# Layer norm, Fourier filter and gated bilinear layer on one core: all sixteen row tiles transposed on TensorE instead of twelve by DMA

## The chip, the cores and the metric

The kernel runs on one core of a Trainium2 chip. The metric is the device time of one execution in microseconds (us). Before the change it is 196.71 us, the median of three runs that lie between 196.61 and 196.75 us.

## The reference

The inputs are bf16. A_x has shape (1, 2048, 640). The reference normalises each of its 2048 rows and adds three terms: the input itself, a filter in the two-dimensional Fourier domain, and a gated bilinear layer.

```python
m = jnp.mean(x, axis=-1, keepdims=True); v = jnp.var(x, axis=-1, keepdims=True)
xn = (x - m) / jnp.sqrt(v + 1e-5)
X = jnp.fft.rfft2(xn.astype(jnp.float32), axes=(-2, -1)) * (w_r + 1j * w_i)   # w: (2048, 321)
a = jnp.fft.irfft2(X, s=(2048, 640), axes=(-2, -1)).astype(jnp.bfloat16)
g = jnp.einsum("bsd,df->bsf", xn, w_gate)     # (640, 1536)
u = jnp.einsum("bsd,df->bsf", xn, w_up)
b = jnp.einsum("bsf,fd->bsd", g * u, w_down)  # (1536, 640)
return x + a + b
```

## The kernel before

**Tiles.** The 2048 rows are sixteen row tiles of 128 rows, held in SBUF in one array of memory (the `arena` of the profile) beside the weights and all intermediate results. PSUM is one tensor `ps` of eight banks.

**Tasks.** `_build` describes the program as tasks: a name, the engines that may run it, a duration that only a planner uses, a function that emits its instructions, and what it reads and writes. `_PLAN` is a list of triples (number of the task, engine, PSUM bank), and `replay` walks through it. So the order of the instructions on each engine, the engine itself where there are two, and the banks are written out by hand in that list. `compute_waits` then derives the semaphore waits. Every engine, SP too, executes its own list strictly in order.

**Names of tasks used below**, with the line that the profile shows, and the work of one task:

- `ld_...` (L675): a load or a store, issued by SP except for the first two on ACT. `ld_x1` to `ld_x3` bring row tiles 1 to 3, `ld_x4` tiles 4 to 7, `ld_x5` tiles 8 to 15; `ld_gw0_0` and `ld_gw0_1` the first gate and up weights, and so on; `ld_fd`, `ld_tf`, `ld_ti`, `ld_g` tables for the Fourier steps; `ld_w...` pieces of the filter; `ld_wd...` parts of w_down.
- Statistics of a row tile, in one of two ways. On DVE: two `bn` (L754) and an `ag` (L761). On ACT: `sm` (L736, the mean) and `sq` (L745, the sum of squares). `act_set` names those of the first four tiles that go to ACT: 2 and 3. Tiles 4 and 5 are on DVE, tiles 6 to 15 on ACT.
- `sd` (L770, L771, ACT): the standard deviation; `rs` (L778, DVE): its reciprocal; `mul` (L795, DVE): subtracts the mean and multiplies, in place. Tiles 0 to 3 have an `sd` each, later tiles one for two.
- `T0_b` (L814, TensorE): five 128x128 transposes of row tile b into PSUM, for tiles 0 to 3 only, and `eT0_b` (L682 on DVE, L681 on ACT), the copy to SBUF. For tiles 0 and 1 that copy is two instructions on DVE.
- `xt_b` (L802, SP): one DMA transpose of row tile b, for tiles 4 to 15. It takes no PSUM and no engine but SP's queue and the DMA engines.
- `GU_f_b_u` (L973 for the narrow ones, L951 for those 512 columns wide): the product of gate (u=0) or up (u=1) weights of column block f with the row tiles that start at b. `eG` is its copy out of PSUM (L681 ACT, L682 DVE), and `H` (L991, L993, DVE) multiplies the two.
- `S1` to `S5` (L857 to L892, DVE), `R_b` (L905, TensorE) and `eR_b`: the first Fourier steps on a row tile. `D`, `C`, `IA`, `I` (L1034, L1053, L1116, L1144) are the further Fourier steps on TensorE, `WM`, `SM`, `J`, `V` those on DVE, ACT and POOL.
- `ACC`, `IV` (L1221, L1233): the product with w_down and the last Fourier step, accumulated in one bank; `FIN` (L1242, L1260) adds the input, and `st_out` stores.
- `warm` (L714) is 42 matmuls on constants ahead of the first useful one, and `fill0` (L704) five more.

**Order around the change.** TensorE begins with

```
warm T0_0 fill0 T0_1 GU_0_0_1 GU_0_0_0 GU_0_1_0 GU_0_1_1 GU_2_0_1 T0_2 GU_2_0_0 T0_3 GU_2_1_0 ...
```

DVE's list begins with the statistics of tile 0, then `bn1`, `bn1`, and only then `rs_0`, `ag1`, `mul0`, `rs_1`, `mul1` and the copies of `T0_0` and `T0_1`. ACT's begins with `sd_0`, `sd_1`, `sm2`, `sq2`, `sm3`, `sd_2`, `sq3`, `sd_3`. SP issues all loads of x and of the gate and up weights first, then `xt4`, `xt7`, `ld_fd`, `xt5`, `xt6`, six filter pieces, and the other eight `xt` scattered among filter pieces and tables.

Of the kernel before, what the change touches and what calls it, by code (L numbers as in the profile page):

```python
# [400 lines left out]
def _d_act(n):  # L401
# [4 lines left out]
    (12, 1, -1), (19, 2, -1), (10, 0, 1), (0, 3, -1), (11, 4, -1), (13, 4, -1), (18, 2, -1), (20, 2, -1), (28, 2, -1),  # L406
    (27, 2, -1), (170, 1, -1), (14, 4, -1), (8, 3, -1), (21, 1, -1), (22, 2, -1), (29, 2, -1), (23, 2, -1), (30, 1, -1),
    (31, 2, -1), (32, 2, -1), (24, 0, 3), (25, 2, -1), (26, 2, -1), (9, 0, 7), (33, 0, 1), (34, 2, -1), (35, 2, -1),
    (181, 0, 0), (182, 2, -1), (36, 1, -1), (37, 1, -1), (15, 4, -1), (43, 1, -1), (38, 1, -1), (169, 4, -1), (179, 0, 6),
    (180, 2, -1), (39, 2, -1), (40, 2, -1), (183, 2, -1), (44, 1, -1), (45, 1, -1), (46, 2, -1), (47, 2, -1), (189, 0, 1),  # L410
    (191, 0, 0), (190, 1, -1), (192, 1, -1), (193, 2, -1), (172, 4, -1), (186, 0, 6), (171, 4, -1), (112, 2, -1), (187, 1, -1),
    (41, 0, 2), (42, 1, -1), (184, 0, 7), (185, 1, -1), (16, 4, -1), (54, 2, -1), (113, 2, -1), (48, 0, 6), (49, 1, -1),
    (62, 1, -1), (194, 0, 5), (196, 0, 3), (197, 1, -1), (195, 1, -1), (188, 2, -1), (198, 2, -1), (50, 2, -1), (51, 2, -1),
    (53, 2, -1), (114, 2, -1), (55, 2, -1), (52, 2, -1), (63, 1, -1), (206, 0, 2), (207, 1, -1), (64, 1, -1), (204, 0, 7),
    (205, 1, -1), (115, 2, -1), (173, 4, -1), (209, 0, 6), (174, 4, -1), (65, 1, -1), (210, 1, -1), (66, 1, -1), (67, 2, -1),
    (56, 1, -1), (57, 2, -1), (116, 2, -1), (199, 0, 3), (200, 1, -1), (70, 2, -1), (201, 0, 2), (202, 1, -1), (203, 2, -1),
    (58, 2, -1), (208, 2, -1), (17, 4, -1), (121, 2, -1), (72, 1, -1), (1, 4, -1), (211, 0, 7), (175, 4, -1), (212, 1, -1),
    (176, 4, -1), (177, 4, -1), (73, 1, -1), (117, 0, 2), (118, 1, -1), (119, 0, 5), (74, 1, -1), (213, 2, -1), (122, 2, -1),
    (68, 2, -1), (123, 2, -1), (75, 1, -1), (76, 1, -1), (77, 2, -1), (216, 0, 1), (217, 1, -1), (214, 0, 0), (215, 1, -1),
    (218, 2, -1), (221, 0, 2), (222, 1, -1), (78, 2, -1), (124, 2, -1), (219, 0, 3), (220, 1, -1), (223, 2, -1), (80, 2, -1),  # L420
    (224, 0, 4), (120, 1, -1), (225, 1, -1), (82, 1, -1), (60, 2, -1), (226, 0, 2), (227, 1, -1), (229, 0, 6), (230, 1, -1),
    (83, 1, -1), (84, 1, -1), (178, 4, -1), (231, 0, 5), (125, 2, -1), (128, 0, 6), (126, 0, 3), (129, 1, -1), (232, 1, -1),
    (228, 2, -1), (130, 2, -1), (233, 2, -1), (131, 2, -1), (59, 4, -1), (71, 4, -1), (2, 4, -1), (236, 0, 0), (237, 1, -1),
    (61, 4, -1), (85, 1, -1), (234, 0, 2), (127, 1, -1), (86, 1, -1), (235, 1, -1), (238, 2, -1), (132, 2, -1), (92, 1, -1),
    (241, 0, 6), (242, 1, -1), (239, 0, 7), (240, 1, -1), (93, 1, -1), (243, 2, -1), (133, 2, -1), (87, 2, -1), (246, 0, 4),
    (244, 0, 1), (245, 1, -1), (94, 1, -1), (247, 1, -1), (248, 2, -1), (134, 2, -1), (69, 4, -1), (249, 0, 6), (250, 1, -1),
    (95, 1, -1), (96, 1, -1), (97, 2, -1), (251, 0, 2), (252, 1, -1), (90, 2, -1), (253, 2, -1), (88, 2, -1), (98, 2, -1),
    (100, 2, -1), (254, 0, 7), (255, 1, -1), (256, 0, 3), (257, 1, -1), (438, 4, -1), (433, 4, -1), (259, 0, 4), (260, 1, -1),
    (258, 2, -1), (137, 0, 5), (139, 0, 0), (437, 4, -1), (435, 4, -1), (441, 4, -1), (472, 4, -1), (101, 4, -1), (91, 4, -1),
    (434, 4, -1), (470, 4, -1), (3, 4, -1), (135, 0, 2), (136, 1, -1), (143, 2, -1), (138, 1, -1), (102, 1, -1), (261, 0, 7),  # L430
    (262, 1, -1), (79, 4, -1), (89, 4, -1), (141, 0, 3), (269, 0, 2), (263, 2, -1), (142, 1, -1), (140, 1, -1), (266, 0, 5),
    (267, 1, -1), (144, 2, -1), (270, 1, -1), (264, 0, 4), (265, 1, -1), (268, 2, -1), (145, 2, -1), (271, 0, 5), (274, 0, 1),
    (103, 1, -1), (104, 1, -1), (272, 1, -1), (273, 2, -1), (81, 4, -1), (442, 4, -1), (466, 4, -1), (146, 2, -1), (105, 1, -1),
    (106, 1, -1), (275, 1, -1), (279, 0, 4), (280, 1, -1), (276, 0, 0), (277, 1, -1), (278, 2, -1), (107, 2, -1), (147, 2, -1),
    (110, 2, -1), (108, 2, -1), (468, 4, -1), (469, 4, -1), (281, 0, 6), (282, 1, -1), (286, 0, 7), (287, 1, -1), (283, 2, -1),
    (284, 0, 3), (152, 0, 4), (148, 0, 6), (153, 1, -1), (99, 4, -1), (431, 4, -1), (440, 4, -1), (432, 4, -1), (4, 4, -1),
    (683, 4, -1), (109, 4, -1), (111, 4, -1), (473, 4, -1), (156, 2, -1), (429, 4, -1), (439, 4, -1), (467, 4, -1), (471, 4, -1),
    (149, 1, -1), (285, 1, -1), (288, 2, -1), (157, 2, -1), (150, 0, 0), (289, 0, 2), (151, 1, -1), (154, 0, 4), (291, 0, 6),
    (296, 0, 0), (290, 1, -1), (292, 1, -1), (155, 1, -1), (293, 2, -1), (158, 2, -1), (301, 0, 2), (299, 0, 6), (300, 1, -1),
    (294, 0, 4), (295, 1, -1), (304, 0, 7), (306, 0, 6), (6, 4, -1), (297, 1, -1), (298, 2, -1), (159, 2, -1), (160, 2, -1),  # L440
    (305, 1, -1), (307, 1, -1), (309, 0, 0), (310, 1, -1), (302, 1, -1), (303, 2, -1), (311, 0, 7), (312, 2, -1), (308, 2, -1),
    (163, 0, 5), (164, 1, -1), (167, 0, 1), (161, 0, 3), (162, 1, -1), (168, 2, -1), (314, 0, 0), (315, 2, -1), (313, 2, -1),
    (165, 0, 4), (316, 0, 6), (317, 2, -1), (166, 1, -1), (446, 0, 2), (447, 1, -1), (448, 2, -1), (474, 0, 0), (443, 0, 4),
    (444, 2, -1), (445, 1, -1), (324, 0, 7), (325, 1, -1), (477, 0, 2), (479, 1, -1), (478, 2, -1), (318, 2, -1), (321, 0, 6),
    (322, 1, -1), (436, 4, -1), (451, 0, 4), (452, 2, -1), (475, 1, -1), (476, 1, -1), (449, 0, 2), (450, 2, -1), (498, 4, -1),
    (503, 4, -1), (504, 4, -1), (497, 4, -1), (534, 4, -1), (453, 2, -1), (319, 0, 7), (320, 1, -1), (323, 2, -1), (454, 2, -1),
    (326, 0, 6), (327, 1, -1), (328, 2, -1), (505, 0, 4), (506, 1, -1), (508, 0, 0), (509, 1, -1), (510, 1, -1), (331, 0, 7),
    (332, 1, -1), (334, 0, 2), (335, 1, -1), (329, 0, 6), (507, 1, -1), (482, 0, 0), (483, 2, -1), (480, 0, 2), (481, 2, -1),
    (484, 2, -1), (455, 1, -1), (330, 1, -1), (341, 0, 7), (342, 1, -1), (336, 0, 4), (337, 1, -1), (456, 3, -1), (457, 3, -1),
    (460, 0, 5), (462, 0, 6), (463, 1, -1), (458, 0, 0), (464, 0, 7), (465, 1, -1), (461, 1, -1), (344, 0, 1), (345, 1, -1),  # L450
    (536, 0, 6), (459, 1, -1), (537, 1, -1), (339, 0, 2), (538, 1, -1), (340, 1, -1), (349, 0, 1), (532, 4, -1), (500, 4, -1),
    (499, 4, -1), (502, 4, -1), (501, 4, -1), (511, 0, 3), (333, 2, -1), (485, 2, -1), (531, 4, -1), (565, 4, -1), (535, 4, -1),
    (560, 4, -1), (530, 4, -1), (528, 4, -1), (529, 4, -1), (513, 0, 6), (351, 0, 0), (486, 2, -1), (350, 1, -1), (352, 1, -1),
    (512, 2, -1), (567, 0, 1), (568, 1, -1), (569, 1, -1), (346, 0, 5), (347, 1, -1), (487, 3, -1), (488, 3, -1), (489, 0, 4),
    (490, 1, -1), (514, 2, -1), (338, 2, -1), (515, 2, -1), (354, 0, 0), (355, 1, -1), (539, 0, 2), (540, 1, -1), (541, 1, -1),
    (493, 0, 1), (491, 0, 6), (492, 1, -1), (494, 2, -1), (356, 0, 4), (357, 1, -1), (359, 0, 7), (360, 1, -1), (517, 2, -1),
    (343, 2, -1), (516, 2, -1), (495, 0, 2), (5, 4, -1), (430, 4, -1), (533, 4, -1), (544, 0, 0), (594, 4, -1), (561, 4, -1),
    (562, 4, -1), (542, 0, 5), (543, 2, -1), (496, 1, -1), (601, 0, 3), (603, 1, -1), (602, 1, -1), (381, 0, 7), (382, 1, -1),
    (366, 0, 2), (367, 1, -1), (545, 2, -1), (348, 2, -1), (593, 4, -1), (519, 3, -1), (518, 3, -1), (526, 0, 6), (527, 1, -1),
# [62 lines left out]
def _build(nc, A_x, A_w_r, A_w_i, B_w_gate, B_w_up, B_w_down, out, opts=None):  # L522
    opts = opts or {}
    tabs = _build_tables()
    es = contextlib.ExitStack()
    with es:
# [21 lines left out]
        b_xta = alloc("XTA", 2 * 2048)  # L548
# [182 lines left out]
        for gi, (b0, nb) in enumerate(_LN_GROUPS):  # L731
# [49 lines left out]
            for b in range(b0, b0 + nb):  # L781
# [18 lines left out]
                if b >= opts.get("xt_dma", 4):  # L800
                    def em_xt(c, b=b):
                        return c.e.dma_start_transpose(v_xt[:, :, b * 128:(b + 1) * 128], v_x[:, b, :])  # L802
# [542 lines left out]
```

## Time and profile before

| | before |
|---|---|
| runs shown | 196.71 us (196.61 to 196.75) |
| profiled execution | 196.57 us |
| its span, first to last instruction | 194.9 us |
| granted TensorE clock, mean | 1.000 |
| ACT busy | 136.4 us (70%) |
| POOL busy | 12.2 us (6%) |

The profile is one execution, taken on the only core. Its span covers the first to the last instruction; the other 1.67 us of the execution lie around it. A page row such as "L951 PE MATMUL ps<-arena 128x512 bf16 x440" is a group of instructions of one source line on one engine, with its total busy time, the mean duration of one, and the idle time of the engine just before them. PEld is the loading of weights into TensorE, which runs beside the matmuls.

### The profile page before, as it was taken

Reading aid. Unit: us, or ns where it says so; the run is one execution under the profiler, and the core shown is the slowest. Engines: PE = TensorE matmul, PEld = TensorE weight load, DVE = VectorE, ACT = ScalarE, POOL = GpSimd, SP = SyncE. Lnnn points to the kernel's source line nnn. Section 1 sums busy time; section 2 is a strip of 40 time slices with the busy share of each in tenths; the row PEclk is TensorE's granted clock in tenths of the full one; section 3 lists DMA queues with packets and bytes.
Section 4 is the critical chain, followed back from the end, with each engine's and each line's share of the span. In section 5 each row is a group of like instructions: output and inputs, shape, how many; then the busy total and the mean of one; then the engine's idle time right before and its main releaser. Section 6 shows DMA issues by size and latency. Waiting matters only on the chain.

```text
span 194.9 us, 4074 instructions
## 1 busy us (share of the span) xinstructions
PE 190.9 (98%) x1568; PEld 120.5 (62%) x1568; DVE 176.7 (91%) x369; ACT 136.4 (70%) x275; POOL 12.2 (6%) x22
## 2 busy tenths in 40 slices
PE   8899999999999999999999999999999999999995
PEld 8797454454454565555655555557777777777774
DVE  3899999999999999999989999987999999999713
ACT  3899999999884679989999999667305523253130
POOL 1000000000000000331031221120000000000000
DMA  5999974016869921366465510005001543135412
GB/s 173 324 370 324 214 98 111 0 37 105 155 130 222 258 68 27 96 145 193 118 153 135 153 36 31 3 0 170 4 0 53 144 143 104 40 95 172 134 68 67
DMA packets 29666, 23.73 MB, mean 122 GB/s; under 512 B 10448, under 2 KB 27600, under 8 KB 29520
## 3 DMA queue, kind: packets, MB, share of 16 engines
q1 hardware_dynamic: 28848, 23.08, 46.5%
q10 hardware_dynamic: 800, 0.41, 0.7%
q8 instruction: 12, 0.20, 0.5%
q14 instruction: 6, 0.05, 0.1%
HBM read 18.89 MB, written 2.62 MB: 110 GB/s over the span
## 4 chain that ended last, share of the span: by engine, by line
PE 95%; DVE 2%; DMA 1%; ACT 1%; issue 0%
PE ps L951 48%; PE ps L1221 27%; PE ps L973 5%; PE ps L1116 3%; PE ps L1034 2%; PE ps L1053 2%; PE ps L905 2%; PE ps L1144 2%; PE ps L1233 2%; DMA arena<-in_A_x_dram 1%; DVE arena L754 1%; PE ps L814 1%; ACT arena L681 1%; DVE arena L682 0%; DVE arena L761 0%
## 5 line engine op out<-in xcount | busy, mean ns | idle before, releaser
L681 ACT ACTIVATE arena<-ps 128x512 bf16<-128x512 f32 (+5 forms) x211 | 111.3, 582 | 48.8 <-PE ps L1233 13.8
L951 PE MATMUL ps<-arena 128*128 128x512 bf16 x440 | 101.9, 379 | 0.0
L951 PEld LDWEIGHTS ps<-arena 128*128 128x128 bf16 x440 | 40.9, 98 | 43.1 <-ACT arena L681 0.9
L1221 PE MATMUL ps<-arena 128*128 128x320 bf16 (+2 forms) x396 | 57.2, 295 | 0.0
L1221 PEld LDWEIGHTS ps<-arena 128*128 128x128 bf16 x396 | 37.6, 98 | 13.2
L1070 DVE TENSOR_TENSOR arena<-ps,arena 128x256 bf16<-128x256 f32 x64 | 22.6, 414 | 1.5 <-PE ps L1053 1.3
L991 DVE TENSOR_TENSOR arena<-arena 128x512 bf16<-128x512 bf16 x44 | 18.7, 426 | 0.6 <-ACT arena L681 0.2
L1260 DVE TENSOR_TENSOR arena<-arena 128x640 bf16<-128x640 bf16 x15 | 7.0, 486 | 5.4 <-ACT arena L681 5.4
L682 DVE CAST arena<-ps 128x512 bf16<-128x512 f32 (+4 forms) x16 | 10.1, 639 | 1.5 <-PE ps L973 0.4
L745 ACT ACTIVATE arena<-arena 128x640 bf16<-128x640 bf16 x12 | 10.2, 849 | 0.1
L682 POOL COPY arena<-arena 64x252 bf16<-64x252 bf16 x8 | 4.1, 510 | 92.8 <-DVE arena L1087 92.5
L973 PE MATMUL ps<-arena 128*128 128x128 bf16 (+1 forms) x120 | 9.5, 237 | 0.3 <-DVE arena L682 0.3
L1116 PEld LDWEIGHTS ps<-arena 128*128 128x128 bf16 x160 | 7.9, 116 | 3.0
L736 ACT ACTIVATE arena<-arena 128x640 bf16<-128x640 bf16 x12 | 9.0, 753 | 0.2
L973 PEld LDWEIGHTS ps<-arena 128*128 128x128 bf16 x120 | 8.4, 98 | 1.1 <-issue 0.4
L1100 POOL TENSOR_SCALAR arena<-arena 64x252 bf16<-64x252 bf16 x8 | 7.5, 943 | 22.9 <-DVE arena L1087 22.6
L1116 PE MATMUL ps<-arena 128*128 128x64 bf16 x160 | 8.3, 198 | 0.0
L1233 PE MATMUL ps<-arena 128*128 128x320 bf16 (+2 forms) x33 | 8.3, 295 | 0.0
L1034 PEld LDWEIGHTS ps<-arena 128*128 128x128 bf16 x160 | 6.4, 98 | 2.7 <-issue 0.5
L857 DVE TENSOR_TENSOR arena<-arena 128x768 f32<-128x768 bf16 (+1 forms) x10 | 7.9, 789 | 0.0
L1073 DVE TENSOR_TENSOR arena<-ps,arena 128x260 bf16<-128x260 f32 x16 | 6.9, 432 | 0.0
L1034 PE MATMUL ps<-arena 128*128 128x64 bf16 (+1 forms) x160 | 6.9, 193 | 0.0
(61 smaller groups left out, 184.3 us busy)
## 6 DMA issues: line engine op xcount, KB each, us to landing
arena<-in_A_x_dram SPq DMA_DIRECT2D x19, 160.0 KB, 2.6
arena<-in_A_w_i_dram SPq DMA_DIRECT2D x30, 80.2 KB, 2.3
arena<-in_A_w_r_dram SPq DMA_DIRECT2D x30, 80.2 KB, 2.3
out_dram<-arena SPq DMA_DIRECT2D x15, 160.0 KB, 1.9
arena<-in_B_w_gate_dram SPq DMA_DIRECT2D x4, 320.0 KB, 6.5
arena<-in_A_x_dram SPq DMA_DIRECT2D x1, 1280.0 KB, 10.8
arena<-c_tf SPq DMA_DIRECT2D x4, 256.0 KB, 4.6
arena<-c_ti SPq DMA_DIRECT2D x2, 512.0 KB, 5.0
```

The costliest lines, as they stand in the source:

```text
L681: return c.e.activation(dst, src, _ACTF.Copy)
L682: return c.e.tensor_copy(dst, src)
L736: return c.e.activation(v_jk, v_x[:, b, :], _ACTF.Copy, scale=1.0 / _D, accum_out=v_m32[:, b:b + 1])
L745: return c.e.activation(v_jk, v_x[:, b, :], _ACTF.Square, scale=-1.0, bias=v_m32[:, b:b + 1], accum_out=v_ss[:, b:b + 1])
L951: ins = c.e.matmul(ps[:, bk, :], v_gw[:, w, j, ft, :], v_xt[:, j, rows], start=(j == 0), stop=(j == 4))
L973: ins = c.e.matmul(ps[:, bk, i * n:(i + 1) * n], v_gw[:, w, j, ft0 + i, :], v_xt[:, j, rows], start=(j == 0), stop=(j == 4))
L991: return c.e.tensor_tensor(v_ht[:, ft0, rows], gb[:, 0, :], gb[:, 1, :], _OP.mult)
L1034: ins = c.e.matmul(ps[:, bk + i, k * 64:k * 64 + n], v_uq[:, k, t + i, :], v_fd[:, k * 128 + w * n: k * 128 + w * n + n], start=True, stop ...
L1070: c.e.tensor_tensor(dst, xh, wv, _OP.mult)
L1116: ins = c.e.matmul(ps[:, bk, 64 * k:64 * k + 64], yl, v_ti[:, q, 0, :], start=True, stop=True)
L1221: ins = c.e.matmul(ps[:, bk, 0:sl3.stop - sl3.start], v_ht[:, ft, a * 128:(a + 1) * 128], v_wd[:, ft, sl3], start=(ft == _FT_ORDER[0]), st ...
L1233: return c.e.matmul(ps[:, bank_of(own), 0:sl3.stop - sl3.start], v_sm[:, 2, :], v_v[:, a, sl3], start=False, stop=True)
```

## The change

All sixteen row tiles take the way of `T0_b` and `eT0_b`; `xt_b` is gone. `act_set` becomes (1, 3), so that the statistics of tile 1 go from DVE to ACT and those of tile 2 from ACT to DVE. `warm` has one matmul more. `_PLAN` is replaced as a whole: the order on every engine, the PSUM banks, and the choice of ACT or DVE for copies are new. The durations changed in the other lines are numbers for the planner and emit nothing.

```diff
 _PLAN = (
-    (12, 1, -1), (19, 2, -1), (10, 0, 1), (0, 3, -1), (11, 4, -1), (13, 4, -1), (18, 2, -1), (20, 2, -1), (28, 2, -1),
...
+    (10, 0, 0), (11, 4, -1), (18, 2, -1), (12, 1, -1), (19, 2, -1), (20, 2, -1), (0, 3, -1), (8, 3, -1), (13, 4, -1),
...
-        nwarm = opts.get("nwarm", 42)
+        nwarm = opts.get("nwarm", 43)
...
-        aset = set(opts.get("act_set", (2, 3))) | set(range(opts.get("act_stats", 6), 16))
+        aset = set(opts.get("act_set", (1, 3))) | set(range(opts.get("act_stats", 6), 16))
...
-                if b >= opts.get("xt_dma", 4):
-                    def em_xt(c, b=b):
-                        return c.e.dma_start_transpose(v_xt[:, :, b * 128:(b + 1) * 128], v_x[:, b, :])
-                    T("xt%d" % b, "sp", 1330.0, em_xt, reads=[(b_x, ("s", b, b + 1))],
-                      writes=[(b_xta, ("s", b * 128, (b + 1) * 128)), (b_xtb, ("s", b * 128, (b + 1) * 128))], prio=pb, nbytes=128)
-                    continue
...
-            wm = T("WM_%d" % t, "dve", 1792.0, em_wm,
+            wm = T("WM_%d" % t, "dve", 1710.0, em_wm,
...
-            T("SM_%d" % t, "dve", 1900.0, em_sm, reads=[(b_pr, ("r", 0, 2))],
+            T("SM_%d" % t, "dve", 1640.0, em_sm, reads=[(b_pr, ("r", 0, 2))],
```

With the numbers of the list put back into names, the engines begin like this:

```
TensorE: warm T0_0 fill0 GU_0_0_1 T0_1 GU_0_0_0 GU_0_1_1 GU_2_0_0 T0_3 GU_0_1_0 T0_2 GU_2_0_1 GU_2_1_1 GU_2_1_0 ...
DVE:     bn0 bn0 ag0 rs_0 mul0 eT0_0 eT0_0 rs_1 mul1 bn2 eT0_1 eT0_1 bn2 rs_3 ag2 mul3 rs_2 H_0_0 mul2 S1_0 ...
ACT:     sd_0 sm1 sq1 sd_1 sm3 sq3 sd_3 eG_0_0_0 eG_0_0_1 sd_2 eG_2_0_0 eG_0_1_1 eT0_3 eG_0_1_0 eT0_2 ...
```

Later on TensorE `T0_7` and `T0_6` come before `R_0`, `T0_4` and `T0_5` around `GU_5_0`, `T0_8` to `T0_15` among the products `GU_3_4` to `GU_8_4`. The new copies `eT0_4` and `eT0_7` are on DVE, the ten others on ACT. TensorE's instructions of every other kind, and those of POOL, are as many as before. On SP `ld_g` and one `ld_tf` move ahead of the last gate and up weights, and `ld_fd` moves from behind `xt7` to a place behind both `ld_ti`, the first of which waits for `mul15`. In this excerpt of SP's list only that move is shown:

```
before: ... ld_gw8_0 ld_gw8_1 xt4 xt7 ld_fd xt5 xt6 ...
after:  ... ld_gw6_1 ld_g ld_tf2 ld_gw8_1 ld_gw8_0 ... ld_ti0 ld_w2_1_0 ld_wd7 (four pieces) ld_ti1 (three pieces) ld_fd ...
```

## The prediction

> **What bounds the kernel now.** I read the busy times first, then the chain that ended last, then TensorE's waits, and last the first 8 us instruction by instruction. The page and a table of two stretches:
>
> ```profile
> PE 190.9 (98%) x1568; PEld 120.5 (62%) x1568; DVE 176.7 (91%) x369; ACT 136.4 (70%) x275; POOL 12.2 (6%) x22
> ...
> PE 95%; DVE 2%; DMA 1%; ACT 1%; issue 0%
> ```
>
> ```profile
> 20.00:62.00 42.00, 42.00 (x234) 20.52 (x232) 42.00 (x83) 37.42 (x81) 0.00 (x0) 1.00 0.65 118
> 62.00:132.00 70.00, 69.91 (x624) 38.71 (x622) 66.28 (x148) 61.75 (x111) 11.63 (x16) 1.00 0.40 100
> ```
>
> The columns after the stretch and its length are busy us of PE, PEld, DVE, ACT and POOL, then clock, DMA share and GB/s. TensorE is busy all of both stretches. Busy is not peak, so the chain in order of time (start, us, what) has to say whether the matmuls run back to back:
>
> ```profile
> 10.27 0.28 PE ps L814 x5
> 10.54 0.56 PE ps L973 x10
> 11.10 0.28 PE ps L814 x5
> ...
> 19.61 8.63 PE ps L951 x40
> ```
>
> Forty matmuls of 512 columns in 8.63 us are 216 ns each, the same as in the rest of the chain (1.08 us for five), at a granted clock of 1.00. TensorE is at its rate. By the starts in the trace it falls behind its own steady pace by only 0.71 us between 12 and 192 us (0.21 at `R_13`, 0.20 at `C_13`, 0.11 at `C_9`, four others under 0.1). The kernel is one dense row of matmuls from 7.31 to 192.5 us, and whatever is added to the row is added to the time.
>
> **The sixty transposes.** The same lines price them: five transposes between dense matmuls take 0.28 us (56 ns each), twice. Twelve times that is **3.36 us**, all in the stretch from 19 to 62 us, where TensorE has no idle time to put them in. The Trainium skill speaks for the change: "VectorE: DVE Perf Modes", section "The three transpose paths", gives 390 ns for a 128x128 transpose on TensorE against 1309 ns by DMA, and its rules advise TensorE where a PSUM destination will do. By 390 ns the sixty would cost 23.4 us and the time would be near 220 us. That is not how they run here: a record lasts 219 ns, but the next starts 56 ns later. I take 0.28 us for five. The comparison is also of the wrong things: of the old way no 1309 ns lie on the chain.
>
> **What goes away.** The DMA transposes' view:
>
> ```profile
> L802 SPq DMA_TRANSPOSE arena<-arena x12: 1199/1276/2637, 19.6 to 58.6; - x12
> ...
> DMA to landing us min/median/max: 2.6/3.8/7.5
> ```
>
> They use 12 x 1.28 = 15 us of SP's queue and some DMA time, and no matmul waits for one. So removing them gains 0 us on the path. What the freed queue could speed up, loads and filter pieces, was waited for only at `R_0` (0.2 us of weight loading for `ld_sm1`, hidden under a running matmul).
>
> **The new copies.** Ten on ACT: the two such copies of before start 0.58 us ahead of their follower, so 5.8 us more. From 20 to 62 us ACT is 37.42 of 42 busy; 43.2 us of work in a stretch that TensorE itself lengthens to 45.4 still fits. Up to 40 us, though, ACT has 0.13 us idle. Only `eT0_6`, `eT0_5` and `eT0_10` stand ahead of ACT's last `sq` (47 us before): 1.74 us more there, against 5 x 0.28 = 1.40 us more of TensorE. The 0.34 us left over is near the margins of before (`eR_7` to `GU_3_4_0` 0.22 us, `eG_6_0_1` to `GU_7_0_1` 0.17 us). Two copies go to DVE, 0.4 us each by the 348 ns of the 384-wide form and 286 of the 256-wide; DVE is full there, but gets 3.36 us of time too. Between 0 and 0.6 us of new waits against up to 0.7 us of old ones that a new order may lose: I take 0 for the middle and the end.
>
> **The start.** Now (start, us):
>
> ```profile
> 4.37 0.89 DVE L754 BATCH_NORM_STATS2 arena<-arena 128x6 f32<-128x320 bf16 x2
> 4.42 0.29 ACT L771 ACTIVATE arena<-arena 128x1 f32<-128x1 f32 x1 [1.34 <-DVE arena L761]
> ...
> 5.18 0.15 DVE L778 RECIPROCAL arena<-arena 128x1 f32<-128x1 f32 x1
> ...
> 5.42 0.39 DVE L795 TENSOR_SCALAR arena<-arena 128x640 bf16<-128x640 bf16 x1
> ```
>
> `sd_0` is done at 4.71, but `rs_0` starts at 5.18, behind tile 1's `bn` pair. With tile 1 on ACT, `rs_0` starts at 4.75, `mul0` at 4.94 and `T0_0` at 5.40 instead of 5.87 (the 43rd warm matmul, 107 ns like the others, is out of the array's way by 5.38 and costs nothing). `T0_0` takes 0.70 and its copies 0.57 as now, so `GU_0_0_1` starts near 6.87 instead of 7.31: 0.44 us gained there. Then it is lost:
>
> - Tile 1 on ACT: `sm1` at 4.77, `sq1` 0.86 later, `sd_1` 0.94 after that (6.57), `rs_1` 6.90, `mul1` 7.10 to 7.54, so `T0_1` at 7.59. TensorE finishes `GU_0_0_1` at 7.43 and waits 0.16. (`GU_0_0_0` behind it also needs gate weights that landed at 7.61, 4.9 us after their issue at 2.67: even a faster tile 1 would gain little.)
> - `GU_0_0_0` runs 7.87 to 8.43. `GU_0_1_1` needs both copies of `T0_1`: its last transpose is out at 8.03, the copies follow at 8.07 and 8.33 (0.26 apart) to 8.62, and a matmul followed such a copy after 0.14: 8.76. TensorE waits **0.33**. Behind that wait stand all other products; nobody else waits for them yet.
> - `T0_3` at 9.88 just finds `mul3` (9.77); `T0_2` at 10.72 just finds `mul2` (10.55), with `sd_2` behind two copies on ACT. `GU_2_2_1` starts at 12.68 against 12.34 now, with the same work done.
>
> So the exchange costs **0.34 us** instead of gaining 0.44; these are the ends of its range. Behind it `R_0` needs `S5_0`, ahead of which three `mul` (0.36 each) now stand on DVE: done at 19.6, TensorE there at 19.76. It fits, barely.
>
> One thing can move the start by itself. The warm matmuls and `T0_0` run 107 ns apart, and only from 6.38 us on 56 ns. "TensorE: Matmul & The Clock Gate", Part 1, has the clock released after some 3.4 us, in a window that does not start with the kernel. Here it took 5.5 us; by the page the flip would be near 4.2 us and an earlier `GU_0_0_1` safe. By the row it comes 0.5 us ahead of the new `GU_0_0_1`; if it slips past, ten matmuls cost up to 0.5 us more, in the slack ahead of `T0_1` first.
>
> **Loads moved.** `ld_g` and `ld_tf2` (416 KB) ahead of the last gate and up weights: at the 345 GB/s of 10 to 20 us, 1.2 us later, 25.6 instead of 24.4 us, for `GU_8_0_0` near 27.4. `ld_fd` goes behind `ld_ti0`, which waits for `mul15` (now 53.6, then about 54.8). At 213 GB/s, the rate of 60 to 70 us, the 2.7 MB from there land by 69.5; `D_0_0` wants them near 70.2. No cost, but 0.7 us from one.
>
> **Sum.** 196.57 (profiled) + 3.36 + 0.34 = 200.27; the median of before is 0.14 above the profiled execution, so **200.4 us**.
>
> **Rivals.**
>
> 1. *The start keeps its gain and the old waits go*: +3.36 - 0.44 - 0.71, **198.9 us**. For it: `rs_0` really stood behind work it doesn't need. Against: tile 1's chain on ACT.
> 2. *Copies or `ld_fd` come late and TensorE starves*: ACT's 5.8 us against 3.36 us of time is 2.4 us if none of its idle time can be used; **202.8 us**. For it: 0.13 us idle up to 40 us. Against: 4.6 us idle by 62 us, and seven of the ten copies are placed late.
> 3. *Faster: the transposes slip into TensorE's gaps* and cost nothing, leaving the start's gain: **196.3 us**. It decides from the point where the gaps between 19 and 62 us exceed about 2.9 us (3.36 less the start's 0.44). The table shows 42.00 of 42.00, the chain matmuls at full pace. Nearly excluded.
>
> **Chances.** Forecast 0.70 (199.5 to 201.3), rival 1 0.10, rival 2 0.17, rival 3 0.03. The range, 199.2 to 202.0, takes in the start's ends and half of rival 2. No change means within 0.2%, or 0.4 us: faster 0.03, same 0.01, slower 0.96.
>
> **What would show it.** L814 with 80 matmuls and TensorE's busy time up by about 3.4 us; five-packs of 0.28 us in the chain; `GU_0_0_1` near 6.9 us, `GU_0_1_1` near 8.8; ACT's and DVE's waits on TensorE not shorter in all. It is wrong if the five-packs cost more than 0.3 us, if TensorE shows idle time over 0.5 us in one place after 12 us, or if the time is under 199 us.

## The result, and the profile after

| | before | changed |
|---|---|---|
| median of the runs shown | 196.66 us (196.42 to 196.75) | 200.91 us (200.79 to 201.59) |
| ratio, 95% interval | | 1.0225 (1.02 to 1.025) |
| profiled execution | 196.57 us | 201.59 us, a second one below: span 199.4 us |

The change costs 4.25 us; the forecast said 200.4 us, that is 3.7 us over its 196.7 us of before. First the page of the changed kernel, the busy row:

```profile
PE 194.2 (97%) x1612; PEld 124.3 (62%) x1629; DVE 180.6 (90%) x376; ACT 138.2 (69%) x280; POOL 12.8 (6%) x22
```

There are 1629 weight loads and only 1612 matmuls: 17 matmul records are missing from this trace. A second run of the same kernel (`after_again`: 201.09 us, 200.77 to 201.64, ratio 1.0237, 1.0216 to 1.0257; its profiled execution took 201.21 us) has all 1629, so I read the changed kernel from that one, except where the first profile is named. Its busy row and its chain:

```profile
PE 194.8 (98%) x1629; PEld 124.2 (62%) x1629; DVE 180.5 (91%) x376; ACT 138.2 (69%) x280; POOL 12.9 (6%) x22
...
PE 70%; DVE 23%; ACT 2%; DMA 2%; issue 1%; SPq 0%
```

TensorE has 61 matmuls more (60 transposes and one warm matmul) and 3.9 us more busy time. The chain no longer stays on TensorE for 95%; it takes DVE for 23%. One should not read more from that than that several engines end level there: between them the row of matmuls is as dense as ever. The groups of the stretch from 20 to 66 us, shapes kept apart, hold the new work:

```profile
L808 PE MATMUL ps<-arena 128*128 128x128 bf16 x50 | 3.9, 219 | 0.0
```

```profile
L682 ACT ACTIVATE arena<-ps 128x512 bf16<-128x512 f32 x38 | 22.2, 633 | 1.9 <-PE ps L945 1.6
...
L682 ACT ACTIVATE arena<-ps 128x640 bf16<-128x640 bf16 x10 | 7.0, 722 | 0.0
```

Fifty of the sixty transposes lie in this stretch. The ten copies on ACT have no idle time ahead of them, and ACT still sits idle 1.9 us ahead of its other copies, 1.6 of them for TensorE: ACT is nearly full, not late. Now the start, in order of time (start, us, engine, line), here from the first profile:

```profile
6.86 0.72 PE L967 MATMUL ps<-arena 128*128 128x128 bf16 x10 [0.47 <-DVE arena L683]
...
7.51 0.45 PE L808 MATMUL ps<-arena 128*128 128x128 bf16 x5
...
7.85 1.33 PE L967 MATMUL ps<-arena 128*128 128x128 bf16 x17
8.00 0.56 DVE L683 COPY arena<-ps 128x384 bf16<-128x384 bf16 x2
```

`GU_0_0_1` starts at 6.86, `T0_1` at 7.51, `GU_0_0_0` at 7.85, and then TensorE waits for both copies of `T0_1`: `GU_0_1_1` starts at 8.62. In the second profile the four starts are 6.86, 7.51, 7.80 and 8.61, the last after a wait of 0.25. There `GU_2_2_1` starts at 12.53 instead of 12.34. The start costs **0.19 us**.

With each matmul put back to its task, the last `IV` starts at 196.88 us instead of 192.34 in before. (The two profiled executions differ by 4.64 us.) These 4.54 us are 3.36 of transposes, 0.19 of the start, and **0.99 that no step of the forecast has**. The largest part of it is one place in the chain in order of time:

```profile
136.53 3.80 DMA arena<-in_B_w_down_dram
140.47 0.57 PE ps L1215 x3
```

The load `ld_wd6`, a part of w_down, is issued at 136.53, behind three loads of input rows on SP, and lands at 140.33; `ACC_3_1_9` needs it and TensorE waits 0.68 us. The kernel before has no such wait: there the same load is issued at 131.79 and lands at 135.12, 1.6 us ahead of its first reader (`ACC_1_1_9`, at 136.74). So the margin was small before, and the new list issues the load 4.7 us later. The other waits behind 12 us that can be named come to 0.91 us against 0.71 before (the longest 0.34 us at `C_15` and 0.24 at `C_4`, against 0.21 at `R_13` and 0.20 at `C_13`).

### The profile page after: what moved, and what is told of

Same layout as the page of the kernel before. It is cut to its first block, busy times and chain, and to the rows that moved or that the text cites. A ratio compares the mean times of both kernels' runs of the same rounds, so it can differ in the third digit from the quotient of the medians.

```text
span 199.8 us, 4175 instructions
## 1 busy us (share of the span) xinstructions
PE 194.2 (97%) x1612; PEld 124.3 (62%) x1629; DVE 180.6 (90%) x376; ACT 138.2 (69%) x280; POOL 12.8 (6%) x22
## 4 chain that ended last, share of the span: by engine, by line
PE 53%; DVE 26%; ACT 12%; DMA 4%; issue 2%; SPq 2%; DVEq 0%
PE ps L945 23%; PE ps L1215 20%; DVE arena L1064 8%; ACT arena L682 7%; DVE arena L985 4%; DVE arena L683 3%; DVE arena L1081 2%; DVE arena L1080 2%; PE ps L715 2%; ACT arena L737 2%; DMA out_dram<-arena 2%; DVE arena L1067 2%; ACT arena L746 2%; DMA arena<-in_B_w_down_dram 2%; PE ps L899 2%
## 5 line engine op out<-in xcount | busy, mean ns | idle before, releaser
L682 ACT ACTIVATE arena<-ps 128x512 bf16<-128x512 f32 (+6 forms) x219 | 116.4, 590 | 52.4 <-PE ps L1227 19.6
L945 PE MATMUL ps<-arena 128*128 128x512 bf16 x423 | 100.0, 379 | 0.9
L683 DVE CAST arena<-ps 128x512 bf16<-128x512 f32 (+3 forms) x16 | 10.4, 658 | 1.8 <-PE ps L945 1.1
L746 ACT ACTIVATE arena<-arena 128x640 bf16<-128x640 bf16 x12 | 10.5, 877 | 0.1
L1094 POOL TENSOR_SCALAR arena<-arena 64x252 bf16<-64x252 bf16 x8 | 8.5, 1059 | 30.1 <-DVE arena L1081 29.8
L737 ACT ACTIVATE arena<-arena 128x640 bf16<-128x640 bf16 x12 | 9.3, 778 | 0.1
L1110 PE MATMUL ps<-arena 128*128 128x64 bf16 x160 | 8.8, 198 | 0.0
```

The lines of the kernel that those rows point to most:

```text
L682: return c.e.activation(dst, src, _ACTF.Copy)
L683: return c.e.tensor_copy(dst, src)
L737: return c.e.activation(v_jk, v_x[:, b, :], _ACTF.Copy, scale=1.0 / _D, accum_out=v_m32[:, b:b + 1])
L746: return c.e.activation(v_jk, v_x[:, b, :], _ACTF.Square, scale=-1.0, bias=v_m32[:, b:b + 1], accum_out=v_ss[:, b:b + 1])
L945: ins = c.e.matmul(ps[:, bk, :], v_gw[:, w, j, ft, :], v_xt[:, j, rows], start=(j == 0), stop=(j == 4))
L1110: ins = c.e.matmul(ps[:, bk, 64 * k:64 * k + 64], yl, v_ti[:, q, 0, :], start=True, stop=True)
```

## The experiments

### Is the added row of transposes the cost?

**The kernel before with sixty more transposes.** Five transposes behind each `R_4` to `R_15`, into a part of PSUM that nobody reads; the DMA transposes and the list stay.

```diff
+                    for j in range(5 if b + u > 3 else 0):
+                        o_ = (bk + 1) * 1024 + 384 + j * 128
+                        ins = c.e.transpose(psb[:, o_: o_ + 128], v_x[:, b + u, j * 128:(j + 1) * 128], v_sm[:, 0, :])
```

> The kernel before with its DMA transposes, its order and its statistics, and 60 more transposes on TensorE, five behind the five matmuls of each of R_4 to R_15, into a part of the PSUM pair that R leaves unused; nothing reads them. Theory (TensorE is a dense row, 56 ns for each transpose): 196.7 + 3.36 = 200.0 us. Rival (the price lies in the copies, the exchange of statistics or the new order, and transposes slip into gaps): 196.7 to 197.2 us.

Measured: 200.14 us (199.76 to 200.21) against 196.48, ratio 1.0179 (1.0162 to 1.0196), 3.66 us more. Its chain in order of time, L905 the R steps and L909 the added transposes:

```profile
40.63 0.28 PE ps L905 x5
40.91 0.28 PE ps L909 x5
41.19 0.28 PE ps L905 x5
41.47 0.28 PE ps L909 x5
```

Each five-pack puts off what follows by 0.28 us, twelve times, 3.36 in all. One more wait, of 0.45 us at `C_7` for a filter piece (its load takes the chain from 89.64 for 6.87 us), is more than the 0.30 us that remain; the wait at `R_13` is 0.11 us instead of 0.21. The transposes cost what the forecast said.

**The same with the copies.** Eleven copies on ACT out of PSUM, 640 columns each, ahead of eleven of the `eR` copies, into columns of SBUF that are free then.

```diff
+                    if b > 3 and c.e is nc.scalar:
+                        copy_on(c, v_ht[:, b - 4, 1408:2048], psb[:, (bk + 1) * 1024 + 384: (bk + 1) * 1024 + 1024])
```

> The same with 11 copies of 640 bf16 from PSUM to SBUF on ACT, one ahead of each eR_4 to eR_14; the last tile has none. The copied values are not used. Theory (ACT has room in a stretch that is 3.36 us longer): 0 to 0.4 us above the kernel with the transposes alone, so 200.0 to 200.4 us. Rival (ACT's copies starve TensorE): 11 x 0.58 = 6.4 us of ACT work less 3.36 us, up to 3 us more, 203 us.

Measured: 203.71 us (203.49 to 204.1), ratio 1.0369 (1.0353 to 1.0385): 3.6 us more than without the copies. A miss. The waits of TensorE and of its weight loads (us in total, times, longest):

```profile
PEld ps L956 <- ACT arena L681: 3.4, 5, 1.2
...
PE ps L956 <- ACT arena L681: 1.5, 3, 0.7
```

TensorE waits for ACT's copies, which the kernel before does not do for more than 0.2 us anywhere. But ACT is not full where most of these waits lie (columns as in the forecast: stretch, its length, busy us of PE, PEld, DVE, ACT, POOL, clock, DMA share, GB/s):

```profile
45.00:66.00 21.00, 19.46 (x119) 9.53 (x118) 18.16 (x30) 17.65 (x35) 0.00 (x0) 1.00 0.83 194
```

ACT is busy 17.65 of 21.00 us there, and TensorE and DVE have idle time too. So I read the 3.6 us not as a matter of how much ACT has to do in all, but of where its list has the copies: each stands ahead of an `eR`, and the copies behind it, for which TensorE waits, come later. Other places for them were not tried in this kernel. The changed kernel has ten such copies and no such wait, in a list that was planned with them. This is the forecast's second rival, seen in another kernel (it gave 202.8 us).

### Is taking it away the same as adding it?

**The changed kernel with 48 transposes less.** One transpose instead of five for each of the tiles 4 to 15; the copies read that one block five times, so that ACT and DVE keep their work.

```diff
-                    for j in range(5):
+                    for j in range(5 if b < 4 else 1):
```

> The changed kernel with one transpose instead of five for each of tiles 4 to 15; the copies keep their size and read that one block five times, so the transposed tiles are incomplete and the products of these rows are wrong. Theory: 48 x 56 ns = 2.7 us less than the changed kernel's 200.9, so 198.2 us. Rival (copies and waits for them carry the loss): 200.4 us or more.

Measured: 201.12 us (200.56 to 201.9), ratio 1.0238 (1.0207 to 1.027). A miss: no gain that the interval shows, where 48 x 56 ns = 2.7 us had been taken off TensorE. My theory of one dense row falls here. The chain of this kernel ahead of `R_12`:

```profile
63.55 0.33 DVE arena L987
63.89 0.60 DVE arena L881
64.49 0.61 DVE arena L882
65.10 0.02 issue
65.13 0.69 DVE arena L887
65.82 0.61 DVE arena L888
66.43 0.14 issue
66.57 1.00 PE ps L901 x15
```

The reader is to see that `R_12` (L901) starts as soon as DVE has ended `S5_4` (L888): DVE sets the pace, and the freed TensorE stands still. The table of the stretches had said so in before already:

```profile
20.00:45.00 25.00, 25.00 (x140) 12.21 (x138) 25.00 (x54) 24.42 (x55) 0.00 (x0) 1.00 0.58 89
45.00:66.00 21.00, 20.95 (x118) 10.14 (x116) 20.79 (x37) 15.64 (x31) 0.00 (x0) 1.00 0.81 174
```

and the second profile of the changed kernel:

```profile
20.00:45.00 25.00, 25.00 (x156) 12.68 (x153) 24.93 (x54) 24.93 (x58) 0.00 (x0) 1.00 0.25 73
45.00:66.00 21.00, 21.00 (x140) 11.19 (x139) 20.86 (x37) 19.05 (x38) 0.00 (x0) 1.00 0.44 126
```

TensorE and DVE are full in both kernels and both stretches, and ACT up to 45 us. The new theory: up to 66 us two or three engines run level, and only taking work from all of them moves the end. Five kernels test it. They combine three cuts: the transposes (above); `mul8` to `mul15` on 64 of 640 columns; and the new copies `eT0_4` to `eT0_15` cut to one of five blocks.

```diff
-                    return c.e.tensor_scalar(v_x[:, b, :], v_x[:, b, :], mean, v_rs[:, b:b + 1], _OP.subtract, _OP.mult)
+                    w_ = 640 if b < 8 else 64
+                    return c.e.tensor_scalar(v_x[:, b, :w_], v_x[:, b, :w_], mean, v_rs[:, b:b + 1], _OP.subtract, _OP.mult)
...
+                    if b > 3:
+                        return copy_on(c, v_xt[:, 0, b * 128:(b + 1) * 128], psb[:, bk * 1024: bk * 1024 + 128])
```

**The short `mul` alone.**

> The changed kernel with mul8 to mul15 on 64 of 640 columns (these tiles are mostly not normalised): DVE is relieved of about 8 x 0.28 = 2.2 us before S5_4. Theory now: up to R_12 the end is set by the later of two full engines, TensorE (66.8 us) and DVE (S5_4 at 66.6). With TensorE's 60 transposes still there it gains no more than the few tenths of waits: 200.5 to 201.0 us. Rival (DVE alone carries the loss): 2 us less, 199 us.

**Fewer transposes and the short `mul`.**

> Both at once: one transpose of five for tiles 4 to 15, and mul8 to mul15 on 64 columns. Theory (two engines level with each other): taking from TensorE alone gave nothing, from DVE alone gives next to nothing, from both gives about 2 us: 199.0 us (198.5 to 199.6). Rival (a third thing sets the pace from 20 to 66 us, ACT's copies or PSUM banks): no more than 0.5 us less than the changed kernel.

**The small copies alone.**

> Leaves out four fifths of each new copy eT0_4 to eT0_15 (only the first of the five 128-column blocks is copied to SBUF, and the products GU of tiles 4 to 15 read that block five times). TensorE and its sixty transposes are as in the changed kernel; ACT has some 10 x 0.4 = 4 us less work, DVE some 0.5 us. Theory (from 20 to 66 us TensorE, DVE and ACT are all full, so that freeing one of them alone gains nothing): 200.7 to 201.2, S5_4 ends near 66.4. Rival (ACT's copies alone set the pace of the changed kernel): 198 or less, S5_4 near 63.

**Fewer transposes and small copies.**

> As after_smallcopy, and tiles 4 to 15 have one transpose each instead of five: TensorE 2.7 us less, ACT some 4 us less, DVE nearly as in the changed kernel. Theory (three full engines): DVE still sets the pace of S1 to S5 and of mul, so 200.2 to 201.0. Rival (only TensorE and ACT are full): 198.4 or less.

**All three.**

> As after_minus48_smallcopy, and mul8 to mul15 work on 64 of 640 columns, so that DVE has some 2.2 us less as well: all three engines have over 2 us less than in the changed kernel. Theory (three full engines, and nothing else): 198.3 to 199.2, S5_4 ends near 64.4, one to two us more than the versions with two of them freed. Rival (something else sets the pace up to 66 us, a DMA or waits in the order of the list that no engine's load explains): 200.2 or more, S5_4 at 66.0 or later. A smaller part of the gain can be lost behind 66 us where a load comes late (ACC_3_1_9 near 140 us); S5_4 tells that apart.

What was really taken away has to be read first, by the groups of the stretch from 20 to 66 us. The short `mul`, in the kernel that has it alone:

```profile
L797 DVE TENSOR_SCALAR arena<-arena 128x64 bf16<-128x64 bf16 x8 | 2.3, 295 | 0.0
...
L797 DVE TENSOR_SCALAR arena<-arena 128x640 bf16<-128x640 bf16 x1 | 0.4, 440 | 0.0
```

A tenth of the columns still takes 295 ns of 440, so DVE loses 8 x 0.145 = 1.2 us and not the 2.2 us that I had written. The small copies, in the kernel that has them alone:

```profile
L682 ACT ACTIVATE arena<-ps 128x512 bf16<-128x512 f32 x37 | 21.7, 605 | 5.0 <-PE ps L947 5.0
...
L682 ACT ACTIVATE arena<-ps 128x128 bf16<-128x128 bf16 x10 | 2.6, 285 | 0.0
```

ACT loses 10 x (722 - 285) ns = 4.4 us, which come back as waits for TensorE (5.0 us instead of 1.6). DVE has two of these copies, at 482 ns in the changed kernel and 216 here: 0.5 us less. The last column but one is the time from the start of `GU_2_2_1` to the end of `S5_4`, which leaves out what the start of the single execution does:

| kernel | off TensorE | off DVE | off ACT | to the end of `S5_4` | median us, ratio to before (interval) |
|---|---|---|---|---|---|
| changed kernel again | 0 | 0 | 0 | 54.06 | 201.09, 1.0237 (1.0216 to 1.0257) |
| short `mul` | 0 | 1.2 | 0 | 54.05 | 201.05, 1.0236 (1.022 to 1.0251) |
| fewer transposes | 2.7 | 0 | 0 | 54.04 | 201.12, 1.0238 (1.0207 to 1.027) |
| small copies | 0 | 0.5 | 4.4 | 54.01 | 200.97, 1.0222 (1.0205 to 1.024) |
| fewer transposes, short `mul` | 2.7 | 1.2 | 0 | 53.75 | 200.51, 1.0206 (1.0191 to 1.0222) |
| fewer transposes, small copies | 2.7 | 0.5 | 4.4 | 53.51 | 200.27, 1.0205 (1.0173 to 1.0236) |
| all three | 2.7 | 1.7 | 4.4 | 52.73 | 199.73, 1.016 (1.0134 to 1.0187) |

Read the column of `S5_4`. A cut in which TensorE or DVE keeps its work gives 0.01 to 0.05 us. Two cuts with a little off both give 0.3 and 0.55. All three give 1.33, somewhat less than what was taken from DVE, the least relieved engine. That is the pattern of level rows: one gains about what the engine that was relieved least has lost. TensorE and DVE are shown to be level; that ACT is as well rests on the kernel with fewer transposes and the short `mul` alone, where 1.2 us off DVE give only 0.31 while ACT keeps its work (there TensorE sits idle 0.85 us ahead of `R_9`, until ACT has done `eG_7_4_0`). The times follow in much the same order, though neighbours in the table overlap in their intervals. Both kernels with small copies and without the short `mul` came within what was expected, the short `mul` alone 0.05 us above it. The expectations for the double cut with the short `mul` (199.0) and for all three (198.3 to 199.2) were too low: for both I had priced the short `mul` at 2.2 us, and in the first I had left ACT out of the theory.

### Where does the rest come from?

**The w_down load earlier.** In the changed list `ld_wd6` is moved ahead of the three loads of input rows.

```
changed: ... ld_xr2 ld_xr0 ld_xr3 ... ld_wd6 ...
here:    ... ld_wd6 ld_xr2 ld_xr0 ld_xr3 ...
```

> The changed kernel with one load moved: ld_wd6, the last piece of w_down, ahead of ld_xr2, ld_xr0 and ld_xr3 on SP instead of behind them. In both profiles of the changed kernel ACC_3_1_9 starts 0.13 us after that load lands and TensorE stands 0.60 and 0.68 us. If the wait is the load's place on the queue, three issues of 0.45 us earlier end it: 0.6 us less, 200.3 us. If other transfers or the copies only take its place, 200.9 us as without.

Measured: 201.24 us (200.76 to 201.59), ratio 1.024 (1.0218 to 1.0262). A miss: nothing is gained. The wait at `ACC_3_1_9` is gone, and in its place the chain has, 23 us later:

```profile
158.72 4.00 DMA out_dram<-arena
162.75 0.45 ACT arena L682
163.24 1.80 PE ps L1215 x12
```

A store has to land before ACT may use its buffer again (`FINA_5_0`, L682), and `ACC_5_1_0` waits 0.65 us for that copy. The store itself goes out behind the `V` and `FIN` steps of DVE, which make up most of this chain from 137.92 to 157 us. In the first profile of the changed kernel both waits stand, with 0.60 and 0.47; in the second only the one for the load. So the wait for the store comes and goes from one execution to the next, and it is not shown that it took the other's place; what would take both away was not tried.

**The start of before in the changed kernel.** The list of before up to `GU_2_2_1`, with tiles 2 and 3 on ACT; the rest of the changed list behind it.

```diff
-        aset = set(opts.get("act_set", (1, 3))) | set(range(opts.get("act_stats", 6), 16))
+        aset = set(opts.get("act_set", (2, 3))) | set(range(opts.get("act_stats", 6), 16))
```

> The changed kernel with the first 77 steps of the list of before (all up to GU_2_2_1) and the statistics of tile 1 on DVE, tile 2 on ACT, as before; from there on the order of the changed kernel. Theory: the exchange costs the 0.20 us by which GU_2_2_1 is later (12.53 against 12.34), and DVE's chain moves with it: 200.7 us. Rival (the exchange is a gain that the transposes hide): 0.3 us or more slower, 201.2 us.

Measured: 201.28 us (201.08 to 201.94), ratio 1.0248 (1.0228 to 1.0267): no gain, a miss. `GU_2_2_1` starts at 12.22, 0.31 us ahead of the changed kernel. But `R_0` starts at 19.77 against 19.62, because it waits for `S5_0` until 19.62: three `mul` that `T0_4`, `T0_6` and `T0_7` need stand ahead of the last step of `S5_0` on DVE. DVE takes back what TensorE had won within 8 us.

**The start of the change in the kernel before.** The same exchange the other way: the changed list up to `GU_2_2_1` and `act_set` (1, 3), the list of before behind it, DMA transposes and all.

> The kernel before with the changed kernel's list up to GU_2_2_1 and its exchange of tiles 1 and 2 (act_set 1, 3); the DMA transposes and the order of everything later stay. Theory (the exchange makes the start 0.2 to 0.34 us later, and R_0 waits for S5_0 on DVE besides): R_0 near 19.4 to 19.7 instead of 18.89, and 0.3 to 0.8 us more than before. Rival (the delay of the start goes into slack ahead of R_0): within 0.2 us of before. Rival of the first rival of the prediction (the start keeps a gain): 0.2 us less or more.

Measured: 197.44 us (197.38 to 197.51) against 196.56, ratio 1.0045 (1.0031 to 1.0059), 0.88 us more. `R_0` starts at 19.88 where 19.4 to 19.7 was expected, the time is 0.88 us longer and not 0.3 to 0.8, and the reason is not the one given. The rows in order of time:

```profile
15.13 0.27 DVE L993 TENSOR_TENSOR arena<-arena 128x256 bf16<-128x256 bf16 x1
...
15.76 1.02 PE L951 MATMUL ps<-arena 128*128 128x512 bf16 x4 [0.77 <-DVE arena L993]
```

`GU_2_2_1` comes 0.26 us late, 0.19 in the changed kernel. Then `GU_4_0_0` waits 0.73 us for `H_2_1` (L993), which stands behind more `bn` work on DVE in the new head, at 15.13 instead of 14.12. (The record of its first matmul is missing; by its weight load, at 15.51, it starts near 15.54.) In the changed kernel `H_2_1` is as late, at 15.05, and nobody waits: there `GU_0_2_0` and `GU_0_2_1` have been put ahead of `GU_4_0_0`. So the exchange of the statistics, with the new order of the head, costs TensorE 0.2 to 0.3 us, and another 0.7 us unless the products behind it are put in a new order too.

## Why the prediction was right, and where not

- **The time.** 200.91 us is within the range and within the forecast's own 199.5 to 201.3; slower, as said with 0.96. The sum forecast was 3.7 us: one term came out 0.15 us too high, and 0.99 us were in no term.
- **The sixty transposes, 3.36 us.** Shown by adding them alone: 0.28 us for five, twelve times. The choice of the row's 56 ns over the 390 ns that the forecast weighs it against decided the forecast, and was right.
- **Nothing gained by taking away the DMA transposes.** No wait of TensorE went with them, and the sum closes without such a gain. Taking them away with nothing in their place was not tried.
- **The copies cost 0.** It holds in the changed kernel: ACT and DVE make TensorE wait 0.04 us between 20 and 66 us. But the margin that I named was a matter of the list and not of ACT's free time: nearly the same copies, put elsewhere, cost 3.6 us beside an ACT that was not full. The two copies on DVE took 0.48 us each and not 0.4.
- **The start, 0.34 us.** 0.19. `T0_1` came at 7.51 and not 7.59, and the wait for its second copy is 0.25 and not 0.33. `T0_0` at 5.38, forecast 5.40, is luck: `mul0`, which was to start at 4.94 and release it, started at 4.81 in the first profile and 4.67 in the second and had ended by 5.26 and 5.11, and `T0_0` follows the last warm matmul after 107 ns in both. So the 43rd warm matmul did hold `T0_0`; the later wait for `mul1` at `T0_1` took that in. `R_0`, which was to come at 19.76 with `S5_0` done at 19.6, came at 19.62 with `S5_0` done at 19.48: it fits barely, as said.
- **The moved loads, no cost.** Right for the two that I worked out: the last gate weights (landed 25.34, said 25.6) and `ld_fd` (landed 66.45, said 69.5).
- **The step that failed: "I take 0 for the middle and the end".** It cost 0.99 us. I followed the loads that the change moves up to 70 us, and not those behind 130 us. `ld_wd6` behind three loads of rows can be read from SP's list, and it had only 1.6 us to spare before. The forecast's own sign that it is wrong, over 0.5 us of TensorE idle in one place after 12 us, came true there. Where most of the 0.99 us lies is shown, and the wait for `ld_wd6` is the load's place in the list; but with that wait gone the kernel was no faster, so what would win the 0.99 us back stays open.
- **"One dense row of matmuls ... whatever is added to the row is added to the time."** Right as a rule for adding, wrong as a picture of the kernel. DVE was as full as TensorE from 20 to 66 us, as my own table showed (42.00 of 42.00 for both up to 62 us). It fits how the time is spent: in the changed kernel the end of `S5_4` comes only 0.92 us later from `GU_2_2_1` on (54.06 against 53.13), about what DVE got in two copies of 0.48 us. Ahead of the first `R` that needs `S5_4` (`R_13` before, `R_12` now) stand 52 of the `GU` products instead of 54. That makes up for 2.16 us of the transposes' 3.36; the missing two products come behind 66 us and are paid there. So the time does not come back when transposes are taken out of the finished list: the order is fixed, the products behind `R_12` can't move up, and `R_12` waits for DVE.

## What to carry to other kernels

Where two engines are level over a stretch, as TensorE and DVE are here, work added to TensorE cost in full, and taking work from one of them gained nothing; so an experiment that adds work and one that takes it away are two different questions, and only both show which rows are level. How busy an engine is doesn't tell by itself what more work on it costs: the eleven copies cost 3.6 us beside an ACT with idle time. In a kernel with a fixed order, work that a full stretch can't hold is pushed behind it; count what stands ahead of the next join in both lists, besides reading waits. A load that a new list puts a few places later is to be followed to its first reader, with the margin that it had before, up to the end of the kernel.

## What the runs showed that was not expected

- A tenth of the columns does not make a tenth of the time: the bf16 `mul` of DVE takes 295 ns for 64 columns and 440 for 640; ACT's copy out of PSUM 285 ns for 128 columns and 722 for 640.
- One list of instructions, executed twice, waits in different places: the first profile of the changed kernel has a wait of 0.47 us for a store at `ACC_5_1_0`, the second has none there.
